# A fifth double step in the third pair of an attention and SwiGLU kernel, with the last quads' attention two visits earlier

## The chip, the cores and the metric

The kernel runs on one core of a Trainium2 chip. The metric is the device time of one execution in microseconds; the median of six runs of the kernel before is 401.4 us.

## What is computed

The reference, cut to its core:

```python
q, k, v: (8, 12, 448, 64)          # batch, heads, sequence, head dimension
attn = sigmoid(q @ k^T / 8 - log(448)) @ v
x = attn, transposed to (8 * 448, 768)
g = x @ w_gate                     # 768 x 1536
out = (g * sigmoid(g) * (x @ w_val)) @ w_out    # w_out: 1536 x 768
```

Attention is elementwise in its sigmoid, so there is no softmax row sum; its output feeds a SwiGLU block. All inputs and the output are float32; inside, the kernel works in bf16 and fp16 with float32 accumulation in PSUM.

## The kernel before, in words

**Attention in quads and visits.** Four heads of one batch form a quad, three quads a batch, 24 quads in all (`NQ`, numbered n). A quad has seven tiles c of 64 keys for each head. For one tile, QK^T (L254) makes 128 x 896 scores in PSUM, and ScalarE's sigmoid (L273, or L270 in two halves) writes them as fp16 into `pt_a`, a ring of ten tiles. When all seven tiles of a quad are there, `pv` (L289) multiplies them with v into one PSUM tile, and VectorE casts the two halves out as `xT` (L304, L312), the transposed input of the block.

Attention is cut into visits: tiles 0 to 3 of a quad, then tiles 4 to 6. The first visit of quad n also runs `pv` of quad n - 1. A visit is put between two units of matrix work of the block.

**The block in pairs of batches.** The eight batches make four pairs pb = 0 to 3. For each pair FFN1 goes over f = 0 to 11, blocks of 128 columns of w_gate and w_val. An ordinary step `ffn1(b, f)` is 12 matmuls for one batch (L324: six for gate, six for value), then a sigmoid on ScalarE (L347) and two VectorE operations (L349, L353) that give `hT`. The pair's FFN2 (L618) follows in four groups of 42 matmuls, or three; it works by a scheme of seven products in place of eight on sums of hT (the S tiles, L539) and sums of w_out.

**Double steps.** For the f listed in `FAST`, FFN1 too uses such a scheme. `double(pb, (f, f + 1))` treats two batches, and gate and value, as a 2 x 2 block product and makes it of seven products of three matmuls, for two f: 42 matmuls (L445) in place of 48. It needs four sums of x (`x_sums`, on GpSimd, L418 to L421) and four sums of weights for each slice of three f (`fast_w`, on VectorE, L397; kind 1 is written in place over w_val). ScalarE copies partial results out (`snap`, L455) and makes two SiLUs; VectorE adds and multiplies (L468, L481, L485, L487, L490). In the kernel before the third pair (pb = 2) has f 0 to 7 in four double steps and f 8 to 11 as ordinary steps, ahead of the double steps; the fourth pair has all twelve f in six double steps. Weight sums and S sums are issued inside double steps as `extra` and by `make_sums`.

**PSUM.** All users share a ring of four tiles of two banks (`ring`, `Banked`). A user that comes round to a tile waits for those that read it last. FFN2 keeps its tile for a whole group.

**Queues.** SyncE issues the loads of q and k, the DMA transposes of the cast q and k (L211), and the stores. GpSimd casts q and k (L204), issues the loads of v, and makes the x sums. What a visit triggers there stands in `plan`: after visit (n, 4), with its sigmoids done (`behind_visit`), quad n + 2 is cast and transposed, its v is loaded, and q and k of quad n + 4 are loaded.

**The order** on each engine is fixed by hand: the units (steps, double steps, parts of FFN2) have nominal durations `FU1` to `FU4`; `PACE` gives nominal times to quads, and a loop puts the next visit ahead of the first unit that starts after its time, if enough nominal time has passed since the last visit:

```python
if visits and tcur >= vtime[0] and not (...) and (vtime[0] < FIRST + 4 or since > (3.8 if len(visits[0]) > 3 else 2.0)):
    seq.append((None, visits.pop(0), 0 if fn is ffn1 else 1))
```

In FFN1 of the second pair this gives a visit of four tiles, a step, a visit of three tiles, two steps, and so on: three steps for a quad. Its 24 steps start with quad 10; quad 18's first visit stands between its last step and FFN2. FFN2 of the second pair holds the visits up to (20, 4), and FFN1 of the third pair those of quads 21 to 23 among its eight ordinary steps.

Of the kernel before, what the change touches and what calls it, by code (L numbers as in the profile page):

```python
# [20 lines left out]
def kernel(  # L21
# [20 lines left out]
    NQ = B * NJ  # L42
    W2 = 2 * S
    LAST = B // 2 - 1
    FAST = {LAST - 1: range(0, 8), LAST: range(NF)}
    hsc = lambda pb: 512.0 if pb in FAST else 4096.0

    qkscale = 1.0 / math.sqrt(D)
# [319 lines left out]

    gT = {}

    def fast_w(s, kind, i=None):

        js = slice(0, JT) if i is None else slice(i, i + 1)
        b11, b21 = wg16[s][:, 0::2][:, js], wg16[s][:, 1::2][:, js]
        b12, b22 = wv16[s][:, 0::2][:, js], wv16[s][:, 1::2][:, js]
        if (s, kind) not in gT:
            n = JT * FW * 128
            at = {3: 0, 2: 1, 4: 2}.get(kind)
            if kind == 1:
                t = wv16[s][:, 0::2]  # L380
            elif s == 0:
                t = half_of(stg_a)[:, at * n:(at + 1) * n]
            elif s == 1 and kind == 3:
                t = half_of(ramp_a)[:, 8 * FW * hw:8 * FW * hw + n]
            elif s == 1:
                t = pt_f[:, (at - 1) * n:at * n]
            elif s == 2:
                t = pt_f[:, (at + 2) * n:(at + 3) * n]
            else:
                t = osp.tile([128, DM], FP32, tag="osb", name=f"g{kind}").bitcast(FP16)[:, :n]  # L390
            gT[(s, kind)] = t if kind == 1 else t.rearrange("p (j n) -> p j n", j=JT)
        t = gT[(s, kind)][:, js]
        a, b, op = {
            3: (b22, b12, SUB), 1: (b12, b11, SUB), 2: (b22, gT.get((s, 1), gT[(s, kind)])[:, js], SUB),
            4: (b21, gT.get((s, 2), gT[(s, kind)])[:, js], SUB),
        }[kind]
        (V if i is None else G).tensor_tensor(out=t, in0=a, in1=b, op=op)  # L397

    pt_f = pt_a.rearrange("p a b s -> p (a b s)")

# [25 lines left out]
    def double(pb, fs, extra=()):  # L426

        b0, b1 = 2 * pb, 2 * pb + 1
        Ds = [Banked("f", made=(pb, f)) for f in fs]
        k = hsc(pb)  # L430
        x = lambda b, odd: lambda j: xT[(b, 2 * j + odd)]
        xs = lambda n: lambda j: xS[(pb, j)][n - 1]
        w = lambda t, odd: lambda f, j: t[f // FW][:, 2 * j + odd, f % FW * 128:(f % FW + 1) * 128]
        ws = lambda kind: lambda f, j: gT[(f // FW, kind)][:, j, f % FW * 128:(f % FW + 1) * 128]
        prods = {
            1: (w(wg16, 0), x(b0, 0)), 2: (w(wg16, 1), x(b0, 1)), 3: (w(wv16, 1), xs(4)), 4: (ws(4), x(b1, 1)),
            5: (ws(1), xs(1)), 6: (ws(2), xs(2)), 7: (ws(3), xs(3)),
        }

        def mm(p, bank, start, stop):  # L440
            for f, D in zip(fs, Ds):
                for j in range(JT):
                    W, X = prods[p]
                    D.write(
                        nc.tensor.matmul(  # L445
                            out=D.t[:, bank, :S], lhsT=W(f, j), rhs=X(j), start=(start and j == 0),
                            stop=(stop and j == JT - 1), skip_group_check=True,
                        ),
                        bank,
                    )  # L450
                yield f, D

        def snap(D, bank, scale, pool, tag):
            o = pool.tile([128, 2, S], FP16, tag=tag, name="snap").rearrange("p a b -> p (a b)").bitcast(FP32)
            D.read(nc.scalar.mul(out=o, in_=D.t[:, bank, :S], mul=scale), bank)  # L455
            return o

        def small(tag):
            return qkT.tile([128, 2, S], FP16, tag=tag, name="small").rearrange("p a b -> p (a b)")

        s1, s2, s5, g, t, v = {}, {}, {}, {}, {}, {}
        for f in fs:
            hT[(pb, f)] = htp.tile([128, 2, S], FP16, tag="hT", name=f"hT_{pb}_{f}")
        for f, D in mm(1, 0, True, False):
            s1[f] = snap(D, 0, 1.0, c16, "c16")
        for f, D in mm(2, 1, True, True):
            g[f] = small("T0").bitcast(FP32)
            D.read(V.tensor_tensor(out=g[f], in0=D.t[:, 1, :S], in1=s1[f], op=ADD), 1)  # L468
        for fn in extra:
            fn()  # L470
        for f, D in mm(6, 0, False, False):
            s2[f] = snap(D, 0, k, v16p, "v16")
        for f in fs:
            t[f] = small("T1")
            nc.scalar.activation(out=t[f][:, :S], in_=g[f], func=SILU)
        for f, D in mm(5, 1, True, False):
            s5[f] = snap(D, 1, k, c16, "c16")
        for f, D in mm(7, 0, False, False):
            v[f] = [tmp.tile([128, S], FP16, tag=tag, name="v") for tag in ("s16", "t1")]
            D.read(  # L480
                V.scalar_tensor_tensor(out=v[f][1], in0=D.t[:, 0, :S], scalar=k, in1=s5[f], op0=MULT, op1=ADD), 0  # L481
            )
        for f, D in mm(3, 1, False, True):
            D.read(
                V.scalar_tensor_tensor(out=v[f][0], in0=D.t[:, 1, :S], scalar=k, in1=s2[f], op0=MULT, op1=ADD), 1  # L485
            )
# [193 lines left out]
    def ffn2_part(pb, moves, by="", extra=()):  # L680

        extra = list(extra)
        for g in moves:
# [3 lines left out]
            if extra:  # L687
                extra.pop(0)()

    FU1, FU2, FU3, FU4 = 2.26, 3.9, 6.83, 7.85  # L690
    units = []
    f1_start, f1_end = {}, {}
    tt = 0.0
    for pb in range(B // 2):
# [8 lines left out]
        for f in FAST.get(pb, ())[::2]:  # L703
            extra = {
                (LAST - 1, 0): ((0, 4), (1, 2)), (LAST - 1, 2): ((1, 4), (2, 3)),
                (LAST - 1, 4): ((2, 1), (2, 2)), (LAST - 1, 6): ((2, 4),),
                (LAST, 0): ((3, 3),), (LAST, 2): ((3, 1),), (LAST, 4): ((3, 2),), (LAST, 6): ((3, 4),),
            }.get((pb, f), ())
            units.append((FU4, double, (pb, (f, f + 1), [lambda a=a: fast_w(*a) for a in extra])))
            tt += FU4  # L710
# [13 lines left out]
        elif pb == 1:  # L724
            part((0, 1, 0, 1), "1")
            part((0,) * 5)
            part((1,) * 5, "", (lambda: list(rest_sums(1, G)),))
            for g in (2, 3):
                part((g,) * 3)
                part((g,) * 4)  # L730
        else:
            part((0, 1) * 7, "1", (skip, lambda: keep_rest(LAST, range(NF), nc.scalar.copy)) if pb < LAST else ())
            if pb == LAST:
                part((3,) * 7)
            part((2,) * 7)
# [2 lines left out]


    FIRST = f1_end[0] - 5.0  # L740
    PACE = ((2 * NJ, FIRST + 3.5), (3 * NJ - 1, FIRST + 28.9), (3 * NJ - 0.5, f1_end[1] - 0.1), (3 * NJ, FIRST + 40.5), (3 * NJ + 2, FIRST + 55.6), (6 * NJ, f1_end[B - 5] - 1.0), (6 * NJ + 0.5, f1_end[B - 5]), (NQ, f1_end[B - 5] + 1.0))
    tiles = [(n, c) for n in range(NJ, NQ) for c in range(C)]
    visits = [tiles[:2], tiles[2:4]]
    for i in range(0, len(tiles), C):
# [173 lines left out]
        plan[(n, 4)] = ((behind_visit, n), (ready, n + 2), (load_v, n + 2)) + ((load_qk, n + 4),) * (n + 4 < NQ)  # L918


    def sums_of_x(pb):
        for j in range(NJ):
            for f in x_sums(pb, j):
                f()

    plan[(NQ - 3, 4)] += ((sums_of_x, LAST - 1),)

    seq = []
    tcur = 3 * FU1
    since, was_v = 99.0, 9  # L930
    was, was_args = ffn1, (0, 2)
    for dur, fn, args in units:
        if visits and tcur >= vtime[0] and not (was is ffn2_part and len(set(was_args[1])) > 1) and not (was is ffn1 and was_args[0] < 2 and was_args[1] == 0) and (vtime[0] < FIRST + 4 or since > (3.8 if len(visits[0]) > 3 else 2.0)):
            seq.append((None, visits.pop(0), 0 if fn is ffn1 else 1))
            vtime.pop(0)
            since, was_v = 0.0, 0
# [6 lines left out]
    for i, (fn, args, _) in enumerate(seq):  # L943
        if fn is ffn1:
            ahead = [len(a) if f is None else 0 for f, a, _ in seq[i + 1:i + 3]] + [0, 0]
            budget[args] = 0 if args == (2 * LAST - 1, 9) else 3 if ahead[0] else 0 if ahead[1] == 4 else 2
        if fn is double:
            args[2].append(lambda: make_sums(5))

# [2 lines left out]
    for fn, args, how in seq:  # L952
# [13 lines left out]
        if pend and (fn is ffn1 and args[1] == 0 and (args[0], NP - 1) not in xT or fn is double or how):  # L966
            for n in pend:
                pv(n)
            pend = []
        if fn is ffn1 and args == (2 * LAST - 2, 8):  # L970
            w2 = [lambda a=a: fast_w(*a) for a in ((1, 3), (1, 1), (0, 3), (0, 1), (0, 2))]
            fill.update({args: w2[:2], (2 * LAST - 1, 10): w2[2:4], (2 * LAST - 1, 11): w2[4:]})
        fn(*args)
        if fn is ffn1 and args == (1, 10):
            behind(hS[last_s[0]][:, :1])
# [44 lines left out]
```

## Time and profile before

| | |
|---|---|
| median of 6 runs | 401.4 us (401.23 to 401.99) |
| the profiled execution, and its span | 401.49 us, 399.7 us |
| DVE, ACT, POOL busy | 250.3, 234.8, 124.3 us |
| FFN1 steps, L324 | 672 matmuls, 148.0 us busy |
| double steps, L445 | 420 matmuls |
| sigmoids of attention, L273 | 148 of 920 ns |
| weight sum of 1152 columns, L397 | about 750 ns |
| S sum of 384 columns, L539 | about 350 ns |
| x sum, L418 to L421 | about 1035 ns |
| granted TensorE clock | 1.00 throughout |

The profile is one execution. Times in its views count from the start of the span; the 1.8 us by which the execution is longer than the span lie around it. Busy shares overlap between engines, so they don't add up; what sets the end is read from the chain that ended last. In a timeline row the columns are start, duration, engine, line, operation, result and operands, and in brackets the idle time ahead of it and what ended that. FFN1 of the second pair runs from about 125 to 204 us, its FFN2 to 239, ordinary steps of the third pair to 267, its double steps from 268 to 300.

### The profile page before, as it was taken

What the parts mean: (1) busy time and instruction counts of PE and PEld (TensorE: products, weight loads), DVE (VectorE), ACT (ScalarE), POOL (GpSimd) and SP (SyncE); (2) the same over time, 40 slices, a digit from 0 to 9 for tenths busy, and PEclk for the clock granted to TensorE, in tenths of its full rate; (3) what the DMA queues carried; (4) which work ended last, traced back from release to release, by engine and by line L of the source; (5) the groups of instructions that cost most, each with busy time, mean ns of one, the idle gap of its engine ahead of it and who ended that gap; (6) DMA issues with size and microseconds to landing.
All of it is one profiled execution on the core that took longest, in us unless ns stands there. A gap on an engine that the chain in (4) does not pass through costs nothing.

```text
span 399.7 us, 8097 instructions
## 1 busy us (share of the span) xinstructions
PE 388.4 (97%) x3116; PEld 201.9 (51%) x3116; DVE 250.3 (63%) x499; ACT 234.8 (59%) x379; POOL 124.3 (31%) x203
## 2 busy tenths in 40 slices
PE   6799999999999999999999999999999999999995
PEld 2345544445555444444455554445556555555653
DVE  2637646688643444466665556479896568887553
ACT  5966785746456777777752667785754055756000
POOL 3629042422311333333333943920007500000900
PEclk9999999999999999999999999999999999999999
DMA  8999979899599777778974899400000520000055
GB/s 248 258 242 259 247 153 252 171 187 120 139 281 233 172 152 172 163 162 100 225 162 105 218 234 171 55 2 0 3 0 2 157 79 2 1 2 0 2 167 149
DMA packets 65575, 54.39 MB, mean 136 GB/s; under 512 B 36033, under 2 KB 61729, under 8 KB 65537
## 3 DMA queue, kind: packets, MB, share of 16 engines
q1 hardware_dynamic: 49744, 38.22, 37.8%
q0 software_dynamic: 15360, 15.34, 24.3%
q8 instruction: 24, 0.39, 0.4%
q10 hardware_dynamic: 432, 0.33, 0.3%
q14 instruction: 15, 0.11, 0.1%
HBM read 47.19 MB, written 11.01 MB: 146 GB/s over the span
## 4 chain that ended last, share of the span: by engine, by line
PE 93%; DMA 3%; DVE 1%; ACT 1%; issue 0%; SPq 0%; POOL 0%; DVEq 0%; ACTq 0%
PE ps_D L324 33%; PE ps_D L618 24%; PE ps_D L445 20%; PE ps_D L289 8%; PE ps_D L254 8%; DMA v<-in_v_dram 2%; DMA st<-in_q_dram 1%; PE ps_D L223 0%; DVE xT L304 0%; DVE xT L312 0%; DVE T L229 0%; ACT pt_a L273 0%; ACT osb L629 0%; DVE t L349 0%; DVE osb L631 0%
## 5 line engine op out<-in xcount | busy, mean ns | idle before, releaser
L273 ACT ACTIVATE pt_a<-ps_D 128x896 f16<-128x896 f32 x148 | 127.3, 920 | 46.8 <-PE ps_D L254 45.8
L324 PE MATMUL ps_D<-xT,wg 128*128 128x448 f16 x336 | 74.3, 353 | 0.3
L324 PE MATMUL ps_D<-xT,wv 128*128 128x448 f16 x336 | 73.7, 352 | 0.0
L349 DVE TENSOR_TENSOR t<-ps_D,s 128x448 f16<-128x448 f32 x56 | 34.9, 624 | 52.0 <-ACT s L347 50.9
L324 PEld LDWEIGHTS <-wg 128*128 128x128 f16 x336 | 30.2, 98 | 36.3 <-issue 12.1
L324 PEld LDWEIGHTS <-wv 128*128 128x128 f16 x336 | 32.8, 98 | 31.0 <-issue 0.6
L455 ACT ACTIVATE snap<-ps_D 128x448 f32<-128x448 f32 x60 | 31.2, 542 | 28.1 <-PE ps_D L445 26.4
L254 PE MATMUL ps_D<-T,T 64*64 64x448 bf16 x644 | 44.3, 357 | 2.1 <-DVE T L229 1.0
L347 ACT ACTIVATE s<-ps_D 128x448 f16<-128x448 f32 x56 | 30.9, 551 | 24.3 <-PE ps_D L324 22.5
L204 POOL CAST c<-stg_a 128x896 bf16<-128x896 f32 x40 | 36.4, 936 | 15.9 <-DMA stg_a<-in_q_dram 14.1
L618 PEld LDWEIGHTS <-S 128*128 128x128 f16 x312 | 30.2, 98 | 20.9 <-issue 1.3
L618 PE MATMUL ps_D<-ramp_a,S 128*128 128x384 f16 x234 | 40.2, 326 | 0.0
L353 DVE SCALAR_TENSOR_TENSOR hT<-ps_D,t 128x448 f16<-128x448 f32 x56 | 35.0, 625 | 5.8
L289 PE MATMUL ps_D<-pt_a,v 64*64 64x448 f16 x672 | 36.0, 350 | 0.9 <-DMA v<-in_v_dram 0.8
L636 DVE SCALAR_TENSOR_TENSOR osb<-ps_D,osb 128x384 f32<-128x384 f32 x42 | 23.4, 557 | 20.0 <-PE ps_D L618 14.6
L631 DVE TENSOR_SCALAR osb<-ps_D 128x384 f32<-128x384 f32 x39 | 21.7, 557 | 20.3 <-PE ps_D L618 16.9
L828 POOL CAST held<-S 128x1 bf16<-128x1 f16 x3 | 0.6, 188 | 100.4 <-ACT osb L629 55.7
L828 POOL CAST held<-pt_a 128x1 bf16<-128x1 f16 x13 | 2.5, 189 | 93.2 <-ACT pt_a L273 93.2
L618 PEld LDWEIGHTS <-hT 128*128 128x128 f16 x228 | 22.1, 98 | 15.6 <-issue 1.3
L254 PEld LDWEIGHTS <-T 64*64 64x64 bf16 x644 | 15.1, 105 | 24.6 <-issue 17.8
L304 DVE CAST xT<-ps_D 128x448 f16<-128x448 f32 x21 | 13.1, 625 | 22.4 <-PE ps_D L289 19.3
L289 PEld LDWEIGHTS <-v 64*64 64x64 f16 x672 | 19.5, 107 | 13.8 <-DMA v<-in_v_dram 1.2
(108 smaller groups left out, 497.1 us busy)
## 6 DMA issues: line engine op xcount, KB each, us to landing
out_dram<-osb SPq DMA_DIRECT2D x52, 192.0 KB, 3.3
stg_a<-in_q_dram SPq DMA_DIRECT2D x18, 448.0 KB, 5.6
stg_a<-in_k_dram SPq DMA_DIRECT2D x18, 448.0 KB, 6.2
v<-in_v_dram POOLq DMA_DIRECT2D x36, 112.0 KB, 4.5
wg<-in_moe_w_gate_dram POOLq DMA_DIRECT2D x4, 576.0 KB, 12.4
wv<-in_moe_w_val_dram POOLq DMA_DIRECT2D x4, 576.0 KB, 13.1
wo<-in_moe_w_out_dram POOLq DMA_DIRECT2D x4, 576.0 KB, 8.8
v<-in_v_dram POOLq DMA_DIRECT2D x6, 224.0 KB, 10.7
```

Source lines behind the costliest of these rows:

```text
L204: eng.tensor_copy(out=t.rearrange("p c h d -> p h c d"), in_=st.rearrange("p h (c d) -> p h c d", c=C))
L254: nc.tensor.matmul(out=sc[g:g + 64, h2, :S], lhsT=kt[r, w * 64:(w + 1) * 64], rhs=qt[r, :, w * 64:(w + 1) * 64], start=True, stop=True,)
L273: nc.scalar.activation(out=pt, in_=sc[:, :, :S], func=SIGM, bias=sbias, scale=qkscale)
L289: nc.tensor.matmul(out=P[g:g + 64, h2, :S], lhsT=vt[r, h2, c * D:(c + 1) * D], rhs=pt[r, h2, :], start=(c == 0), stop=(c == C - 1),)
L324: nc.tensor.matmul(out=D.t[:, i, :S], lhsT=(wg16, wv16)[i][f // FW][:, pr, cs], rhs=xT[(b, pr)], start=(pr == 0), stop=(pr == NP - 1),),
L347: D.read(nc.scalar.activation(out=s16, in_=D.t[:, 0, :S], func=SIGM), 0)
L349: D.read(nc.vector.tensor_tensor(out=t1, in0=D.t[:, 0, :S], in1=s16, op=MULT), 0)
L353: nc.vector.scalar_tensor_tensor(out=hT[(b // 2, f)][:, b % 2, :], in0=D.t[:, 1, :S], scalar=hsc(b // 2), in1=t1, op0=MULT, op1=MULT),
L445: nc.tensor.matmul(out=D.t[:, bank, :S], lhsT=W(f, j), rhs=X(j), start=(start and j == 0), stop=(stop and j == JT - 1), skip_group_check=True,
L455: D.read(nc.scalar.mul(out=o, in_=D.t[:, bank, :S], mul=scale), bank)
L618: nc.tensor.matmul(out=D.t[:, bank, :hw], lhsT=l, rhs=B_(i), start=(first and i == order[0]), stop=(i == order[-1]), skip_group_check=True,),
L636: D.read(nc.vector.scalar_tensor_tensor(out=o, in0=i, scalar=1.0 / hsc(pb), in1=o, op0=MULT, op1=ADD), bank)
```

## The change

- f 8 and 9 of the third pair become a fifth double step. The pair keeps f 10 and 11 as ordinary steps: four where there were eight.
- `PACE` moves quads 18 and later one quad on relative to the nominal end of FFN1 of the second pair, and the loop's minimum distance ahead of a four-tile visit falls from 3.8 to 2.0 from quad 12 on. In the order that results, FFN1 of the second pair holds 15 visits from (12, 0) on where it held 13: (12, 0) to (18, 4), with (19, 0) between its last step and FFN2. FFN2 of the second pair holds the visits up to (21, 4), FFN1 of the third pair those of quads 22 and 23, one ahead of each step. Between (11, 4) and (13, 0) stand three steps, and four between (n, 4) and (n + 2, 0) elsewhere in this stage; before there were five.
- The fourth slice of weights is cut in two for its sums (`gcut`): f 9 alone (384 columns a sum), f 10 and 11 (768 columns). The sums for f 9 are made in double steps of the third pair, for f 10 and 11 in the fourth pair.
- Two weight sums of the second slice move from FFN1 of the third pair into FFN2 of the second pair, group 3; the x sums of the third pair are issued after FFN2 of the second pair and not by `plan` of quad 21.
- One special budget of S sums goes.

```diff
-    FAST = {LAST - 1: range(0, 8), LAST: range(NF)}
+    FAST = {LAST - 1: range(0, 10), LAST: range(NF)}
...
+    gcut = [(i, 0, FW) for i in range(NW - 1)] + [(NW - 1, 0, 1), (NW - 1, 1, FW)]
+    def gpart(f):
+        return next(i for i, (s, lo, hi) in enumerate(gcut) if s == f // FW and lo <= f % FW < hi)
+    def fast_w(i, kind):
+        s, lo, hi = gcut[i]
+        cs = slice(lo * 128, hi * 128)
+        b11, b21 = wg16[s][:, 0::2, cs], wg16[s][:, 1::2, cs]
+        b12, b22 = wv16[s][:, 0::2, cs], wv16[s][:, 1::2, cs]
+        n = JT * (hi - lo) * 128
...
+            elif i == 3:
+                o = JT * FW * 128 * 5 + NF * 128
+                t = pt_f[:, o + at * n:o + (at + 1) * n]
...
+        V.tensor_tensor(out=t, in0=a, in1=b, op=op)
...
-                (LAST - 1, 4): ((2, 1), (2, 2)), (LAST - 1, 6): ((2, 4),),
-                (LAST, 0): ((3, 3),), (LAST, 2): ((3, 1),), (LAST, 4): ((3, 2),), (LAST, 6): ((3, 4),),
+                (LAST - 1, 4): ((2, 1), (2, 2)), (LAST - 1, 6): ((2, 4), (3, 3), (3, 1), (3, 2)),
+                (LAST - 1, 8): ((3, 4),),
+                (LAST, 0): ((4, 3),), (LAST, 2): ((4, 1),), (LAST, 4): ((4, 2),), (LAST, 6): ((4, 4),),
...
-            for g in (2, 3):
-                part((g,) * 3)
-                part((g,) * 4)
+            part((2,) * 3)
+            part((2,) * 4)
+            part((3,) * 3, "", (skip, lambda: fast_w(1, 3), lambda: fast_w(1, 1)))
+            part((3,) * 4)
+            o_units.append((0.0, sums_of_x, (LAST - 1,)))
...
-    PACE = (..., (6 * NJ, f1_end[B - 5] - 1.0), (6 * NJ + 0.5, f1_end[B - 5]), (NQ, f1_end[B - 5] + 1.0))
+    PACE = (..., (6 * NJ + 1, f1_end[B - 5] - 1.0), (6 * NJ + 1.5, f1_end[B - 5]), (NQ, f1_end[B - 5] + 1.0))
...
-    plan[(NQ - 3, 4)] += ((sums_of_x, LAST - 1),)
...
-        if visits and ... since > (3.8 if len(visits[0]) > 3 else 2.0)):
+        if visits and ... since > (3.8 if len(visits[0]) > 3 and visits[0][0][0] < 4 * NJ else 2.0)):
...
-            budget[args] = 0 if args == (2 * LAST - 1, 9) else 3 if ahead[0] else 0 if ahead[1] == 4 else 2
+            budget[args] = 3 if ahead[0] else 0 if ahead[1] == 4 else 2
...
-        if fn is ffn1 and args == (2 * LAST - 2, 8):
-            w2 = [lambda a=a: fast_w(*a) for a in ((1, 3), (1, 1), (0, 3), (0, 1), (0, 2))]
-            fill.update({args: w2[:2], (2 * LAST - 1, 10): w2[2:4], (2 * LAST - 1, 11): w2[4:]})
+        if fn is ffn1 and args == (2 * LAST - 2, 10):
+            w2 = [lambda a=a: fast_w(*a) for a in ((0, 3), (0, 1), (0, 2))]
+            fill.update({(2 * LAST - 1, 10): w2[:2], (2 * LAST - 1, 11): w2[2:]})
```

More of the change, by code (lines that the diff above doesn't have):

```diff
@@ L369 @@
     gT = {}
[L371 to L381, printed above, removed]
+    gcut = [(i, 0, FW) for i in range(NW - 1)] + [(NW - 1, 0, 1), (NW - 1, 1, FW)]
@@ new lines, in gpart @@
+    def gpart(f):
[6 more added lines that the diff above has]
+        n = JT * (hi - lo) * 128
+        at = {3: 0, 2: 1, 4: 2}.get(kind)
+        if kind == 1:
+            t = b12
+        else:
+            if i == 0:
@@ L382, in fast_w @@
                 t = half_of(stg_a)[:, at * n:(at + 1) * n]
-            elif s == 1 and kind == 3:
+            elif i == 1 and kind == 3:
                 t = half_of(ramp_a)[:, 8 * FW * hw:8 * FW * hw + n]
-            elif s == 1:
+            elif i == 1:
                 t = pt_f[:, (at - 1) * n:at * n]
-            elif s == 2:
+            elif i == 2:
                 t = pt_f[:, (at + 2) * n:(at + 3) * n]
+            elif i == 3:
+                o = JT * FW * 128 * 5 + NF * 128
+                t = pt_f[:, o + at * n:o + (at + 1) * n]
@@ L389, in fast_w @@
             else:
                 t = osp.tile([128, DM], FP32, tag="osb", name=f"g{kind}").bitcast(FP16)[:, :n]
-            gT[(s, kind)] = t if kind == 1 else t.rearrange("p (j n) -> p j n", j=JT)
-        t = gT[(s, kind)][:, js]
+            t = t.rearrange("p (j n) -> p j n", j=JT)
+        gT[(i, kind)] = t
         a, b, op = {
-            3: (b22, b12, SUB), 1: (b12, b11, SUB), 2: (b22, gT.get((s, 1), gT[(s, kind)])[:, js], SUB),
-            4: (b21, gT.get((s, 2), gT[(s, kind)])[:, js], SUB),
+            3: (b22, b12, SUB), 1: (b12, b11, SUB), 2: (b22, gT.get((i, 1)), SUB), 4: (b21, gT.get((i, 2)), SUB),
@@ L396, in fast_w @@
         }[kind]
-        (V if i is None else G).tensor_tensor(out=t, in0=a, in1=b, op=op)
+        V.tensor_tensor(out=t, in0=a, in1=b, op=op)
     pt_f = pt_a.rearrange("p a b s -> p (a b s)")
@@ L433, in double, with ws, at @@
         w = lambda t, odd: lambda f, j: t[f // FW][:, 2 * j + odd, f % FW * 128:(f % FW + 1) * 128]
-        ws = lambda kind: lambda f, j: gT[(f // FW, kind)][:, j, f % FW * 128:(f % FW + 1) * 128]
+        def ws(kind):
+            def at(f, j):
+                i = gpart(f)
+                lo = (f % FW - gcut[i][1]) * 128
+                return gT[(i, kind)][:, j, lo:lo + 128]
+            return at
         prods = {
@@ L688, in ffn2_part, with sums_of_x @@
                 extra.pop(0)()
+    def sums_of_x(pb):
+        for j in range(NJ):
+            for f in x_sums(pb, j):
+                f()
     FU1, FU2, FU3, FU4 = 2.26, 3.9, 6.83, 7.85
@@ L740 @@
     FIRST = f1_end[0] - 5.0
-    PACE = ((2 * NJ, FIRST + 3.5), (3 * NJ - 1, FIRST + 28.9), (3 * NJ - 0.5, f1_end[1] - 0.1), (3 * NJ, FIRST + 40.5), (3 * NJ + 2, FIRST + 55.6), (6 * NJ, f1_end[B - 5] - 1.0), (6 * NJ + 0.5, f1_end[B - 5]), (NQ, f1_end[B - 5] + 1.0))
+    PACE = ((2 * NJ, FIRST + 3.5), (3 * NJ - 1, FIRST + 28.9), (3 * NJ - 0.5, f1_end[1] - 0.1), (3 * NJ, FIRST + 40.5), (3 * NJ + 2, FIRST + 55.6), (6 * NJ + 1, f1_end[B - 5] - 1.0), (6 * NJ + 1.5, f1_end[B - 5]), (NQ, f1_end[B - 5] + 1.0))
     tiles = [(n, c) for n in range(NJ, NQ) for c in range(C)]
@@ L918 @@
         plan[(n, 4)] = ((behind_visit, n), (ready, n + 2), (load_v, n + 2)) + ((load_qk, n + 4),) * (n + 4 < NQ)
[L921 to L924, printed above, removed]
-    plan[(NQ - 3, 4)] += ((sums_of_x, LAST - 1),)
     seq = []
@@ L932 @@
     for dur, fn, args in units:
-        if visits and tcur >= vtime[0] and not (was is ffn2_part and len(set(was_args[1])) > 1) and not (was is ffn1 and was_args[0] < 2 and was_args[1] == 0) and (vtime[0] < FIRST + 4 or since > (3.8 if len(visits[0]) > 3 else 2.0)):
+        if visits and tcur >= vtime[0] and not (was is ffn2_part and len(set(was_args[1])) > 1) and not (was is ffn1 and was_args[0] < 2 and was_args[1] == 0) and (vtime[0] < FIRST + 4 or since > (3.8 if len(visits[0]) > 3 and visits[0][0][0] < 4 * NJ else 2.0)):
             seq.append((None, visits.pop(0), 0 if fn is ffn1 else 1))
```

## The prediction

> **What bounds the kernel now.** I read the page first, then the chain that ended last, then the timelines at three places that the change alters.
>
> ```profile
> PE 388.4 (97%) x3116; PEld 201.9 (51%) x3116; DVE 250.3 (63%) x499; ACT 234.8 (59%) x379; POOL 124.3 (31%) x203
> ...
> PE 93%; DMA 3%; DVE 1%; ACT 1%; issue 0%; SPq 0%; POOL 0%; DVEq 0%; ACTq 0%
> ```
>
> TensorE works 97% of the span and carries 93% of the chain. A matmul removed shortens the end; a wait added to TensorE lengthens it. In order of time the chain prices every unit that the change moves:
>
> ```profile
> 137.15 0.69 PE ps_D L254 x12
> 137.84 4.65 PE ps_D L324 x24
> 142.49 0.50 PE ps_D L254 x8
> 142.99 1.32 PE ps_D L289 x28
> 144.31 0.38 PE ps_D L254 x8
> 144.69 2.38 PE ps_D L324 x12
> ...
> 268.06 31.89 PE ps_D L445 x168
> ```
>
> The visit to a quad's last three tiles costs 0.69 us; the visit to the first four, with the earlier quad's PV inside, 0.50 + 1.32 + 0.38 = 2.20. One FFN1 step behind a visit costs 2.38, a second one 4.65 - 2.38 = 2.27. Four double steps of 42 matmuls take 31.89, 7.97 each. I write (n,0) for the visit to tiles 0 to 3 of quad n and (n,4) for the one to tiles 4 to 6.
>
> **The gain.** Four steps become one double step: 4 x 2.27 = 9.08 against 7.97, so -1.11 us (six matmuls of 0.19 give the same). The number of visits stays, so their cost moves and doesn't change.
>
> **First new wait: quad 13's transposes.** Before, five FFN1 steps always stand between (n,4), whose plan casts and transposes quad n+2, and (n+2,0), which reads it. The order of the changed kernel has four, and between (11,4) and (13,0) only three. On TensorE that stretch is 0.69 + 2.38 + 2.20 + 2.38 + 0.69 + 2.38 = 10.72 us. The other chain, in the timeline from (11,4) on:
>
> ```profile
> 137.08 0.76 PE L254 MATMUL ps_D<-T,T 64*64 64x448 bf16 x12
> 137.52 2.54 ACT L273 ACTIVATE pt_a<-ps_D 128x896 f16<-128x896 f32 x3 [0.67 <-PE ps_D L254]
> ...
> 139.92 0.56 ACT L347 ACTIVATE s<-ps_D 128x448 f16<-128x448 f32 x1
> ...
> 140.30 1.81 POOL L204 CAST c<-stg_a 128x896 bf16<-128x896 f32 x2
> ...
> 141.25 0.62 DVE L353 SCALAR_TENSOR_TENSOR hT<-ps_D,t 128x448 f16<-128x448 f32 x1
> 141.26 1.28 SPq L211 DMA_TRANSPOSE T<-c  x1
> ```
>
> Three sigmoids, then the hold behind them, two casts, two transposes. The second is issued at 142.64 (the first at 141.26, 1.28 of issue and a gap of 0.1). Its own entry in the view of tile T, and that of the slowest one, at 182.4:
>
> ```profile
> DMA to landing us min/median/max: 5.8/5.8/5.8
> ```
> ```profile
> DMA to landing us min/median/max: 7.3/7.3/7.3
> ```
>
> So k of quad 13 lands at 148.44, while TensorE wants it at 137.08 + 10.72 = 147.80. With about 0.1 for the semaphore and the weight load, the wait is 0.7 us. The same entry reads 5.2 in the slots at 152.5 and 172.3; that would make it 0.1. 7.3 would make it 2.2. I take 5.8: up to 140.15 this very slot has the same instructions in both kernels. All other shortened stretches have four steps, 13.0 us against 11.4, and keep over 1.5 us; a stall at quad 13 only adds to that. The next narrowest is quad 23: the slot that will hold its second transpose lands at 239.92 + 5.9 = 245.8, and (23,0) is due at 239.12 + 2.20 + 2.38 + 0.69 + 2.38 = 246.77. 1.0 us is left; no cost, but 0.5 at 7.3.
>
> The Trainium skill, "DMA: Bandwidth & Descriptors", section "Issuing engines are not separate DMA queues", says that transfers issued by SP and POOL run on the same 16 DMA engines and interleave. This speaks against closer visits, since the loads of one quad then run into the transposes of the next; at 182.4 the v, q and k transfers of that slot are as late as its transposes, which fits. The page gives no price for it.
>
> **Second new wait: the start of FFN2 of the second pair.** Before, two FFN1 steps run ahead of the last visit, (18,0); after, (18,4), one step, (19,0). The second FFN2 group takes the PSUM buffer that held the PV result, and its first matmul waits for both DVE casts out of it (ps_D_99 in the order of both kernels). Before:
>
> ```profile
> 202.36 0.62 DVE L353 SCALAR_TENSOR_TENSOR hT<-ps_D,t 128x448 f16<-128x448 f32 x1
> ...
> 204.03 0.62 DVE L304 CAST xT<-ps_D 128x448 f16<-128x448 f32 x1 [0.24 <-PE ps_D L289]
> ...
> 204.57 0.61 DVE L312 CAST xT<-ps_D 128x448 f16<-128x448 f32 x1
> ```
>
> With the visit's start at 202.08 as zero, the casts end at 3.10, and the group begins at 3.20 (2.20 for the visit, 0.98 for the first group's six matmuls): 0.1 to spare. After, the last gate follows a three-tile visit, as at 137.08 above: there hT starts 4.17 after that visit, which is 4.17 - 3.07 = 1.10 after the next one. Three S sums follow on DVE (0.54, 0.92 and 1.20 after hT's start, as at 192.44), the casts start 1.47 and 2.01 after it, and the second ends at 1.10 + 2.01 + 0.61 = 3.72. TensorE waits 3.72 + 0.07 - 3.20 = 0.59 us. Bounds: 0.50 and 0.65, by the semaphore and DVE's spacing.
>
> **Smaller waits.** In the first double step s5's copy (ACT L455) ended 0.08 ahead of the matmul that needs its bank, of which 0.05 is the semaphore. Upstream, DVE's `small` started at 270.47, 2.81 after hT's at 267.66. Now the two S sums in between depend on the hT just made and on each other, where before one was ready: 0.66, 1.05, then 1.32 (weight sum), 1.99 and 2.53 (casts), 3.07. That is 0.26 late; less the slack, 0.18 (0.1 to 0.25). In the double step for f 6, 7, DVE has four weight sums (one of 1152 columns, three of 384) and four S sums between `small` and L481, where the busiest one had two and four and left 0.08 us. By rows (1152: 0.75, 384: 0.35) and the waits among the three I get 3.0 to 3.3 us of room needed from 294.92 and 3.2 available: 0 to 0.15, I take 0.05. One stall goes: the 0.09 before the second step behind a three-tile visit (at 167.7), a place that a visit now breaks up.
>
> The skill's "VectorE: DVE Perf Modes", section on the TRN2 errata, holds that an SBUF operation pays a fixed cost per instruction, and advises tiles of 512 and more, which speaks against cutting a weight sum of 1152 into 384 and 768. The rows agree in kind: 0.75 and 0.35 make 0.15 fixed. Its expression (58 + half the columns at 0.96 GHz) gives an estimate of 0.26 for 384 columns; by that the double step for f 6, 7 would not wait at all.
>
> **What costs nothing, and its cover.** POOL's 12 x-sums (1.03 each, 12.4) start at about 240.6, wait for the stores of FFN2's last group (landing by 247.6) and end before 254; the first double step is due at 239.12 + 16.75 = 255.9 and reads them 2.3 later. Each us beyond 4 of delay would be paid. The two weight sums put into FFN2's fourth group (0.75 each) push one PSUM copy by 0.3, and that bank is next written after a 0.69 visit and a 0.98 product. The closer visits' sigmoids: the sequence four-tile visit, step, three-tile visit, step, four-tile visit stood already at 44 to 57 us, where the chain is PE alone. Loads of q and k have two quads' time (over 20 us) against 6.2 to land, and SP keeps transposes ahead of the fourth group's stores as before. The fifth double step in itself is like the others.
>
> **The sum** against the profiled execution's 401.49 (span 399.7 and 1.8 around it, 0.1 above the median of 401.4): -1.11 - 0.09 + 0.70 + 0.59 + 0.18 + 0.05 = +0.32. On the median: 401.7 us.
>
> **Rivals.**
> A (forecast, 0.60): the gain is paid back in waits; with 5.2 to 5.9 at quad 13 and the smaller bounds, -0.5 to +0.65, 400.9 to 402.1.
> B, the covers hold (0.15): quad 13's transposes land at 5.2 or sooner and FFN2's casts are not needed so early, so 0.3 us of waits remain: 401.4 - 0.9 = 400.5. For: of the thirteen slots from 119 us on, ten have 5.1 to 5.6 for the second transpose. Against: the FFN2 wait is made of DVE rows that hardly vary.
> C, slower (0.25): the transposes of the closer quads land late, as at 182.4. Quad 13 then waits 2.2 (1.5 more), quad 23 0.5: 401.7 + 1.5 to 2.0, about 403.4. It decides from 6.3 us to land, where the total passes +0.8. For: the DMA share is 0.80 over 122 to 205 us, at 9.92 us for a quad; at 7.65 it is full. Against: quad 13's slot itself has yet no closer neighbour.
> That the change would not do what it says is out: the order shows 3110 matmuls for 3116, and (19,0) ahead of FFN2.
>
> **The numbers.** A measurement of this kernel tells 0.2%, 0.8 us, from no change: 400.6 to 402.2. A gives 0.57 to no change and 0.03 to slower, B 0.10 to faster and 0.05 to no change, C 0.21 to slower and 0.04 to no change: faster 0.10, same 0.66, slower 0.24. Range for 8 in 10: 400.6 (B's middle) to 403.0 (C's lower part).
>
> **What would show it.** Matmuls of L445 x462 in all, the page's count 3110; in the chain a DMA piece of T ahead of L254 at about 148 (quad 13), 0.1 to 0.8 long, and a DVE xT piece ahead of L618 at about 208; a short ACT snap piece in the first double step at about 257; no POOL xS piece. Wrong if neither wait shows and the span is 398.6, or if transposes stand in the chain at several quads.

## The result, and the profile after

The changed kernel took 402.67 us (median of 16 runs, 402.11 to 404.22) beside 401.49 for the kernel before (37 runs): ratio 1.0031, 95% interval 1.0024 to 1.0037, so 1.2 us slower. Compared again with the same kernel before on two other occasions, it was at 1.0017 (1.0008 to 1.0025) and 1.0022 (1.0012 to 1.0031). It is slower each time, by 0.7 to 1.2 us, about at the 0.2% that I had called the limit of what can be told. The forecast of 401.7 with "no change" as the likeliest case was too low by one microsecond; the time lies in the upper part of the stated range, 400.6 to 403.0.

The matmuls are gone as foreseen, in the first line of busy times:

```profile
PE 388.7 (97%) x3110; PEld 201.6 (50%) x3110; DVE 253.0 (63%) x505; ACT 237.5 (59%) x385; POOL 123.6 (31%) x203
```

TensorE's busy time nevertheless rose from 388.4 to 388.7. A second profile of the kernel before (before_again below) has 391.1, so the busy times of the page don't tell where the loss is. The chain that ended last, in order of time (start, length, what), holds the larger ones:

```profile
208.91 0.54 DVE xT L312
209.45 0.04 issue
209.50 7.97 PE ps_D L633 x48
...
260.21 4.66 PE ps_D L460 x24
264.87 0.03 ACTq L470
264.90 0.65 ACT small L490 x2
265.55 0.44 ACT snap L470
265.99 0.04 issue
266.04 34.21 PE ps_D L460 x180
300.25 20.48 PE ps_D L633 x126
320.72 47.67 PE ps_D L460 x252
...
380.26 3.31 DMA out_dram<-osb
...
383.69 0.57 DVE osb L646
384.26 0.04 issue
384.30 11.87 PE ps_D L633 x72
```

Three places where TensorE is released by another engine, where the chain of before was TensorE alone: the start of FFN2 of the second pair (209.50), the first double step (266.04) and the last FFN2, where a copy waits for a store to land (384.30). The first two were in the forecast, the third was not.

A table of stages says what each is worth. It counts from the first matmul of the second pair's FFN1, because the start-up ahead of that varies between executions: in the 14 profiles of this study that matmul starts anywhere from 124.2 to 126.0 us. The stages are taken from the starts of TensorE's matmuls in the trace; the last one ends with its last matmul.

| us | before | before, again | changed | changed, again | changed, third |
|---|---|---|---|---|---|
| FFN1, 2nd pair | 79.59 | 79.59 | 83.08 | 83.09 | 83.08 |
| FFN2, 2nd pair | 36.97 | 36.97 | 37.65 | 37.66 | 37.65 |
| ordinary steps, 3rd pair | 26.73 | 26.73 | 14.66 | 14.66 | 14.67 |
| double steps, 3rd pair | 31.79 | 31.79 | 39.94 | 39.95 | 39.94 |
| FFN2, 3rd pair | 20.48 | 20.48 | 20.48 | 20.47 | 20.48 |
| double steps, 4th pair | 47.67 | 47.67 | 47.67 | 47.67 | 47.67 |
| FFN2, 4th pair | 27.46 | 27.46 | 27.93 | 27.57 | 28.22 |
| from the start of FFN1, 2nd pair, to the end of the span | 275.01 | 275.02 | 275.73 | 275.39 | 276.05 |

Outside the last FFN2 the stages repeat to 0.01 us. The first six rows sum to +0.25 us, the last FFN2 adds 0.11 to 0.76: 0.4 to 1.0 in the spans.

### The profile page after: what moved, and what is told of

Same layout as the page of the kernel before. It is cut to its first block, busy times and chain, and to the rows that moved or that the text cites. A ratio compares the mean times of both kernels' runs of the same rounds, so it can differ in the third digit from the quotient of the medians.

```text
span 400.5 us, 8109 instructions
## 1 busy us (share of the span) xinstructions
PE 388.7 (97%) x3110; PEld 201.6 (50%) x3110; DVE 253.0 (63%) x505; ACT 237.5 (59%) x385; POOL 123.6 (31%) x203
## 5 line engine op out<-in xcount | busy, mean ns | idle before, releaser
L324 PE MATMUL ps_D<-xT,wg 128*128 128x448 f16 x312 | 69.2, 353 | 0.2
L324 PE MATMUL ps_D<-xT,wv 128*128 128x448 f16 x312 | 68.5, 352 | 0.0
L349 DVE TENSOR_TENSOR t<-ps_D,s 128x448 f16<-128x448 f32 x52 | 32.4, 624 | 53.6 <-ACT s L347 53.1
L470 ACT ACTIVATE snap<-ps_D 128x448 f32<-128x448 f32 x66 | 34.1, 541 | 29.5 <-PE ps_D L460 27.6
L324 PEld LDWEIGHTS <-wg 128*128 128x128 f16 x312 | 27.8, 98 | 34.0 <-issue 12.1
L324 PEld LDWEIGHTS <-wv 128*128 128x128 f16 x312 | 30.4, 98 | 28.8 <-issue 0.6
L347 ACT ACTIVATE s<-ps_D 128x448 f16<-128x448 f32 x52 | 28.7, 552 | 22.8 <-PE ps_D L324 21.1
L353 DVE SCALAR_TENSOR_TENSOR hT<-ps_D,t 128x448 f16<-128x448 f32 x52 | 32.5, 625 | 5.4
L460 PE MATMUL ps_D<-xS,wv 128*128 128x448 f16 x132 | 28.6, 352 | 0.0
L460 PE MATMUL ps_D<-xT,wg 128*128 128x448 f16 x132 | 26.8, 353 | 0.0
```

The source lines that it names most:

```text
L324: nc.tensor.matmul(out=D.t[:, i, :S], lhsT=(wg16, wv16)[i][f // FW][:, pr, cs], rhs=xT[(b, pr)], start=(pr == 0), stop=(pr == NP - 1),),
L347: D.read(nc.scalar.activation(out=s16, in_=D.t[:, 0, :S], func=SIGM), 0)
L349: D.read(nc.vector.tensor_tensor(out=t1, in0=D.t[:, 0, :S], in1=s16, op=MULT), 0)
L353: nc.vector.scalar_tensor_tensor(out=hT[(b // 2, f)][:, b % 2, :], in0=D.t[:, 1, :S], scalar=hsc(b // 2), in1=t1, op0=MULT, op1=MULT),
L460: nc.tensor.matmul(out=D.t[:, bank, :S], lhsT=W(f, j), rhs=X(j), start=(start and j == 0), stop=(stop and j == JT - 1), skip_group_check=True,
```

## The experiments

The theory after the first profile: the step's 1.11 us is paid back by waits that the closer visits make (FFN2's start, and small ones at many visits) plus something at the end. The rivals: transposes that land late in unprofiled executions (C of the prediction), and a double step that is worth less than its matmuls in that place.

**casts_first**, the FFN2 wait alone. The S sums of the last step are not issued behind the step, and so come behind the casts:

```diff
-            budget[args] = 3 if ahead[0] else 0 if ahead[1] == 4 else 2
+            budget[args] = 0 if args == (2 * LAST - 3, NF - 1) else 3 if ahead[0] else 0 if ahead[1] == 4 else 2
```

> The changed kernel with one reordering on DVE: the three S sums behind the last FFN1 step of the second pair are held back, so that the two casts xT of the last visit's PV result come ahead of them. If the wait at the start of FFN2 is a real price of the closer visits (my second term, 0.59; the trace of the changed kernel shows 0.52 of idle TensorE there and a first FFN2 stretch of 9.56 us for 8.88), the idle time goes and the first stretch falls back to about 8.9: 0.5 to 0.7 us below the changed kernel, 402.0 on the median and span 399.9. Rival 1, the wait only hides another one behind it (a store of that group, the next PSUM bank): the gap moves by less than 20 us and the time stays at 402.6. Rival 2, the loss comes from transposes that land late in some executions: the time stays at 402.4 to 402.7 and its spread stays as wide (402.1 to 404.2).

Measured 401.64 us (ratio 1.0000, 0.9991 to 1.0008), FFN2 of the second pair 36.96. Its chain has no cast at FFN2's start any more, and it has quad 13's transposes:

```profile
142.40 5.41 DMA T<-c
147.81 0.04 issue
147.85 0.57 PE ps_D L254 x8
...
207.75 8.89 PE ps_D L633 x54
```

The first stretch of FFN2 is 8.89 us again for 54 matmuls, as before the change. For comparison, the chain of the kernel before:

```profile
204.36 8.90 PE ps_D L618 x54
```

So the wait is shown, at 0.69, and nothing hides behind it. Rival 1 falls with that. This one profile lost 0.35 of the gain elsewhere: FFN1 of the second pair took 83.25 for 83.08 (the wait for quad 13's transposes) and the last FFN2 28.11 for 27.93. The median fell by more than 0.69 and the spread narrowed (401.3 to 402.2), so that rival 2, a second cause in unprofiled executions, was not out of the question: the changed kernel itself had to be measured again. Against its later two ratios the step is 0.7 to 0.9, which leaves little for it.

**visits_alone**, the visits of the changed kernel, but four double steps:

```diff
-    FAST = {LAST - 1: range(0, 10), LAST: range(NF)}
+    FAST = {LAST - 1: range(0, 8), LAST: range(NF)}
-    gcut = [(i, 0, FW) for i in range(NW - 1)] + [(NW - 1, 0, 1), (NW - 1, 1, FW)]
+    gcut = [(i, 0, FW) for i in range(NW)]
```

and the weight sums in the double steps as in the kernel before.

> The changed kernel's visit positions with four double steps as before, so four ordinary FFN1 steps in place of the fifth double step. If the double step itself is worth its 1.11 us and the loss comes from the visits (FFN2 start 0.6 to 0.7, seven or eight visits at 0.08 to 0.12 each, perhaps 0.5 at the end), this kernel is slower than the kernel before by 1.2 to 1.9 us, 402.7 to 403.4, and 0.9 to 1.1 above the changed kernel less what the first double step loses there (0.1 to 0.2). If instead the double step is worth much less in that place (its weight sums and copies hold it up), this kernel is about as fast as the changed one, 402.4 to 402.7, that is 0.9 to 1.2 above before. If the visits cost nothing, it is within 0.2 of before.

Measured 404.04 us (1.0052, 1.0040 to 1.0065), slower than any theory allowed. The chain ahead of its first double step runs through VectorE:

```profile
268.37 0.68 DVE stg_a L402
...
271.83 0.73 DVE stg_a L402
272.56 0.05 issue
272.61 29.68 PE ps_D L457 x156
```

Weight sums stand there beside four ordinary steps that no longer have visits between them, and TensorE idles for 1.06 us. That was the edit's own fault, and it decides nothing about the visits; visits_alone_2 mends it.

**quad13_later**, one more step ahead of quad 13's two visits:

```diff
+    at_13 = next(i for i, g in enumerate(visits) if g[0] == (13, 0))
+    vtime[at_13] = max(vtime[at_13], f1_start[2] + 8 * FU1 - 0.1)
+    vtime[at_13 + 1] = max(vtime[at_13 + 1], f1_start[2] + 9 * FU1 - 0.1)
```

> The changed kernel with the two visits of quad 13 one FFN1 step later, so that four steps stand between (11,4) and (13,0) as at the other quads, and one of the seven tight places (three-tile visit, one step, four-tile visit) is gone. If the transposes of quad 13 bind in most executions but not in the profiled one (rival C or my first term at 0.70), the median falls by 0.3 to 0.8 from the changed kernel's, to 401.9 to 402.4, and the spread narrows to the 0.9 us that most executions keep. If they don't bind, only the tight visit's 0.08 goes: 402.5 to 402.6, the same spread.

Measured 402.13 us (1.0009, 1.0000 to 1.0018). FFN1 of the second pair took 83.00, 0.08 less: the price of one tight place (three-tile visit, a single step, four-tile visit) and no more. The median alone fitted the late transposes; a repeat beside the changed kernel follows below (quad13_again).

**spread_visits**, positions by hand for quads 10 to 19, in steps from the start of FFN1:

```diff
+    starts = (0, 2, 5, 8, 10, 13, 16, 18, 21, 24)
+    for i, grp in enumerate(visits):
+        n, c = grp[0]
+        if 10 <= n <= 19 and (n, c) < (19, 1):
+            vtime[i] = f1_start[2] + (starts[n - 10] + (c > 0)) * FU1 - 0.1
```

Besides, the loop's minimum distance of 3.8 ahead of a four-tile visit now ends with quad 9 and not with quad 11.

> The changed kernel with the visits of quads 10 to 19 placed by hand, three FFN1 steps to a quad: four-tile visit, one step, three-tile visit, two steps; only three places keep the tight pattern, every (n,4) has at least four steps to (n+2,0), and two steps stand ahead of the last visit (19,0). The same number of visits and steps as in the changed kernel. If the loss is the sum of the FFN2 wait (0.6 to 0.7) and of the tight visits at 0.08 (four of seven go, 0.3), it falls by 0.9 to 1.0, to 401.6, the time before; with the wait at the end of the run gone too, if that is chance, to 401.2. If the tight visits cost nothing of their own, it is 402.0. If the loss is at the double step, it stays at 402.5.

Measured 401.45 us (0.9996, 0.9985 to 1.0006). FFN1 of the second pair 82.75 (four tight places fewer, 0.33 less, so 0.08 each), its FFN2 36.96 (the wait gone by the order of the visits alone). Both prices of the theory stand.

**changed_again**, the changed kernel with no edit.

> The changed kernel itself, once more, beside the next three. Its runs lay 1.2 us above the kernel before, and its one profile 0.8 above, while holding back three S sums took 1.2 off where the profile's idle time was 0.66. If the waits seen in single profiles come and go by chance (quad 13's transposes, absent in the first profile and 0.17 with the sums held back; the store at the end, 0.31 and 0.49), another profile of the same kernel shows another mix of them, with a span between 400.0 and 400.9, and the median is 0.7 to 1.2 above before. If the first measurement stands as it is, the median is again 1.1 to 1.4 above and a wait that neither profile shows is to be looked for.

Measured 402.15 us (1.0017). The two waits that vary are indeed absent from its chain: quad 13's product starts only 0.09 late, and the last FFN2 is one piece, 0.11 longer than before the change:

```profile
368.35 27.42 PE ps_D L633 x168
```

**visits_alone_2**, visits_alone with the weight sums moved beside visits:

```diff
-        if fn is ffn1 and args == (2 * LAST - 2, 10):
+        if fn is ffn1 and args == (2 * LAST - 2, 9):
...
-            fill.update({(2 * LAST - 1, 10): w2[:2], (2 * LAST - 1, 11): w2[2:]})
+            fill.update({args: w2[:1], (2 * LAST - 2, 10): w2[1:2], (2 * LAST - 2, 11): w2[2:]})
```

> The closer visits with four double steps, as in visits_alone, but the three weight sums that stood on DVE beside the last two ordinary steps of the third pair (with no visit next to them there, they kept TensorE idle for 1.06 us ahead of the first double step) are put beside the visits of quads 22 and 23. If that pile-up was a fault of my experiment, the gap goes and the kernel is 1.3 us above before (0.50 + 0.68 + 0.12 from the stages), 402.8 to 403.1; the changed kernel less this one is then what the fifth double step brings, net of its own waits: -1.11 + 0.20 + 0.3 to 0.5 at the end, -0.4 to -0.6. If the pile-up stays (S sums alone suffice), it is again 402.1 in span and 2.1 above before.

Measured 402.74 us (1.0030, 1.0018 to 1.0042), 1.27 above before. In its chain the pile-up is gone:

```profile
259.86 9.19 PE ps_D L324 x48
269.04 31.78 PE ps_D L457 x168
...
368.97 27.31 PE ps_D L630 x168
```

Four ordinary steps and four double steps take 9.19 + 31.78 = 40.97 us, where the changed kernel's chain has 300.25 - 260.21 = 40.04 for its five: the fifth double step is worth 0.93, about its 1.11 less 0.20 at the first double step. The theory that it is worth less falls. In time the changed kernel beside it is 0.59 faster, within the 0.4 to 0.6 expected; the visits cost 1.28 in the span (276.29 for 275.01), and the last FFN2 has no wait with four double steps.

**stores_split**, two queues for the first stores of the last FFN2:

```diff
-            store((nc.sync, nc.sync), *rows[0], o1, both)
+            store((nc.sync, nc.scalar if pb == LAST and g < 2 else nc.sync), *rows[0], o1, both)
```

> The changed kernel with one edit at the end: of the two halves of the first stores of groups 0 and 1 in the last FFN2, ScalarE's queue issues the second (SyncE's issued both). In all four kernels with five double steps the second of these issues takes 0.91 to 1.34 us, in both kernels with four 0.59; the copy that needs the buffer waits for its landing, and TensorE for the copy (0.31 idle in the changed kernel). If the serial issue on SyncE is the cause, the idle time goes and the last FFN2 falls from 27.9 to 27.5 us: 0.3 to 0.5 below the changed kernel run beside it. If the landing itself is late in these kernels whatever issues it, the last FFN2 stays at 27.7 to 28.1.

Measured 402.10 us (1.0021, 1.0011 to 1.0030), no gain over the changed kernel beside it. The last FFN2 fell to 27.46, but the time from its last matmul to the end rose from 4.32 to 4.59, and changed_again, profiled beside it, had little wait to lose (0.11). In time the edit is inconclusive.

**spread_split**, spread_visits with the split stores and, by the same means as in casts_first, the S sums of the last ordinary step of the third pair held back.

> All that the stages point to together: the visits spread by hand (as in spread_visits), the split stores of stores_split, and the S sums of the last ordinary step of the third pair held back, so that the first double step finds the PV casts done (0.20 us there in each kernel with five double steps). From spread_visits' span of 399.63: less 0.5 at the end (gap) and 0.2 at the first double step, 398.9 to 399.1, and a median of 400.7 to 400.9, 0.8 to 1.0 below before. If the held sums only move the wait into a later double step, 401.0; if the store stays late, 401.3.

Measured 400.77 us (0.9987, 0.9978 to 0.9996), 0.7 below before and the fastest version of the study. Its chain has a plain FFN2 start, five double steps at 7.97 and a plain end:

```profile
206.98 8.90 PE ps_D L633 x54
...
258.61 39.83 PE ps_D L460 x210
...
366.59 27.32 PE ps_D L633 x168
```

**before_again**, the kernel before with no edit, as a control.

> The kernel before, timed against itself and profiled once more. It prices two things: what the comparison makes of no change (ratio 1.000, within 0.1%), and whether its last FFN2 (27.46 us, no wait for a store) and its quad 13 vary from execution to execution. If a store's issue of 0.9 us or more near 380 us is a matter of chance in any kernel, it can show here too; if it belongs to five double steps, this profile has issues of 0.47 to 0.60 again, as the two kernels with four have had so far.

Measured 401.79 us, ratio 1.0003 (0.9992 to 1.0015): no change is told as no change. Its stages are in the table, its store issues in the last FFN2 take 0.47 to 0.60.

**changed_third** and **quad13_again**, side by side.

> The changed kernel a third time; its two comparisons gave 1.2 and 0.7 us above before, its profiles 0.8 and 0.4. What stays in every profile (tight visits 0.60, FFN2 start 0.68, quad 23 0.12, first double step 0.20, less 1.11 and 0.09) is 0.4; the rest comes and goes. If that is all, the median is again 0.5 to 1.2 above before, and the profile's span 400.1 plus whatever chance wait it holds at quad 13 (0 to 0.2) or at the end (0 to 0.5).

> quad13_later beside the changed kernel on one chip. In six profiles with quad 13 early its second transpose landed at most 0.1 us ahead of the product that needs it, and 0.17 behind the need in one. If it is late by more in many unprofiled executions (rival C), this kernel's median is 0.5 or more below the changed kernel's of the same call; if the wait is the 0 to 0.2 that the profiles show, 0.1 to 0.3 below (0.08 of it the tight visit).

Measured 402.42 us for both, with ratios of 1.0022 (1.0012 to 1.0031) and 1.0014 (1.0005 to 1.0023). The medians are equal and the ratios differ by 0.3 us, well within their intervals. That speaks against late transposes that cost unprofiled executions half a microsecond or more; with 12 runs of each kernel it doesn't exclude it.

**spread_held**, spread_split without the split stores.

> spread_split without the split stores: visits spread by hand and the S sums of the last ordinary step of the third pair held back, SyncE issues all stores. If the split stores were worth the 0.5 us of the end wait, it is 401.2 to 401.3, half a microsecond above spread_split; if that wait is chance, 400.8 to 401.0. Either way 0.2 to 0.7 below before.

Measured 401.35 us (0.9993, 0.9982 to 1.0004). From the start of FFN1 of the second pair its span is 274.48, 0.53 below before; spread_split's is 274.32. The first matmul of that FFN1 came the latest of all profiles, 1.3 us behind the first one's, which hides the gain in the span. The last FFN2 was 27.89 here and 27.46 with split stores, a longer end takes back 0.27 of that. Only spread_split is faster than before beyond its interval.

## Why the prediction was right or wrong

**The gain, -1.11: right.** 40.97 against 40.04 us is 0.93, and the 0.20 of the first double step comes on top.

**FFN2's start, +0.59: right in place and cause, small by 0.1.** The stage grew by 0.68.

**The first double step, +0.18: right, 0.20.** The chain has the short ACT pieces that were expected, though from 264.90 and not at about 257. This double step starts at 260.14, not at the 255.9 of the prediction, which had left out that two visits now stand ahead and that the waits add up (3.49 and 0.68 in the table); the copy comes 5.3 us into it. Holding the sums back takes the wait away (39.74 in spread_held and spread_split for 39.94). The 0.05 at f 6, 7 did not appear: every later double step takes 7.94.

**Quad 13, +0.70: wrong in size.** The step that failed is the landing. Timeline and tile view of the changed kernel:

```profile
147.92 0.57 PE L254 MATMUL ps_D<-T,T 64*64 64x448 bf16 x8
```
```profile
DMA to landing us min/median/max: 4.8/4.8/4.8
```

I had taken 142.64 + 5.8 = 148.44 against a need at 147.80 to 147.9. The second transpose was issued later, at 143.05, but landed 4.8 after that, at 147.82, just in time. In the three profiles of the changed kernel it took 4.6 to 5.0. The product started 0.29 us after the step's last matmul in two of them and 0.37 in changed_again, where 0.28 is usual: waits of 0.01 and 0.09, the latter in place of a 0.08 described below. In casts_first the landing took 5.4 and TensorE idled for 0.17. These are about the lower of my bounds, 0.1. The reason I gave for the middle one, the same instructions in the slot before the change, doesn't reach far enough: this slot has 5.8 and 6.3 in the two profiles of the kernel before. What else makes the difference, no run isolates. **Rival C** goes with it. Over 119 to 243 us the transposes of the changed kernel land in

```profile
DMA to landing us min/median/max: 3.0/4.8/6.6
```

against 5.2 and 7.3 for median and maximum before. Closer visits did not make them later. The rule that I had set beside this (the Trainium skill, "DMA: Bandwidth & Descriptors", section "Issuing engines are not separate DMA queues", on transfers that interleave on the same engines whoever issues them) may hold, but no run here shows it costing the transposes anything.

**"What costs nothing": wrong by 0.7 us for the closer visits.** The x sums, the two weight sums and the fifth double step were free as foreseen: none of them stands in the chain. But I had let the closer visits pass because the same sequence stood at 44 to 57 us, where the chain is TensorE alone. The row that I leaned on had the price in it. From the chain of before:

```profile
45.95 0.38 PE ps_D L254 x8
...
52.27 1.32 PE ps_D L289 x28
53.60 0.46 PE ps_D L254 x8
54.05 2.38 PE ps_D L324 x12
```

The visit at 51.77 is the one behind the tight pattern, and its last piece is 0.46 instead of 0.38. So short a wait stays inside the chain's TensorE piece and only makes it longer. The cause is in the timeline of the changed kernel:

```profile
167.69 0.56 ACT L347 ACTIVATE s<-ps_D 128x448 f16<-128x448 f32 x1
168.28 0.62 DVE L349 TENSOR_TENSOR t<-ps_D,s 128x448 f16<-128x448 f32 x1 [2.48 <-ACT s L347]
168.31 1.49 PE L289 MATMUL ps_D<-pt_a,v 64*64 64x448 f16 x28
169.01 0.62 DVE L353 SCALAR_TENSOR_TENSOR hT<-ps_D,t 128x448 f16<-128x448 f32 x1
169.69 0.57 PE L254 MATMUL ps_D<-T,T 64*64 64x448 bf16 x8
```

The step's sigmoid stands behind three attention sigmoids on ScalarE (165.28 to 167.82), so hT is late and ends at 169.63; the visit's second half of QK needs that PSUM tile and starts 0.06 later, 1.38 after PV began instead of 1.32. Seven of the nine visits in that stage pay this. The stage grew by 3.49; the two visits that moved in are 0.69 + 2.20, with 0.11 for each step that now stands first behind a visit 3.11; 0.38 remain. That is seven times 0.08 less the stall that went, which was 0.16 and not my 0.09: before the change 0.44 us lie between the last matmul of the visit (167.25) and the step's first (167.69), where 0.28 is usual. (23, 0) pays another 0.12.

**The end: not in the sum at all.** I costed the last FFN2 at nothing because no edit touches it. It grew by 0.11 to 0.76 in every kernel with five double steps whose stores are issued by SyncE alone (eight profiles), and in no kernel with four (four profiles). The SP timeline shows two issues in 1.68 us after the change, 1.10 before, the second 1.16 instead of 0.59:

```profile
379.74 1.68 SPq L565 DMA_DIRECT2D out_dram<-osb  x2
```
```profile
379.44 1.10 SPq L550 DMA_DIRECT2D out_dram<-osb  x2
```

What lies beside it is a load of instructions, on queue q8 of the page (24 a run, 0.39 MB). In the DMA view, one load starts between 379.7 and 380.2 of the changed kernel and one between 378.5 and 379.0 of the kernel before:

```profile
q8 instruction: 1, 0.02, 15.7%
```
```profile
q8 instruction: 1, 0.02, 16.6%
```

By the trace's DMA records the one after the change starts at 379.80 and takes 1.25 us; the store's issue ends at 381.42, 0.37 behind it. In all eight profiles the long issue is the one that is open when that load ends, and it ends 0.37 to 0.38 later. In the seven of them where it is the second issue, the growth of the stage is the time of this issue less 0.68 to 0.70: its length reaches TensorE one for one. Counted from the first matmul of the last FFN2 the load starts 10.6 to 10.8 us in with four double steps; with five and SyncE's stores it is 11.5 to 11.7 in six profiles and 12.2 to 12.3 in two. Six matmuls fewer, with their six weight loads, shift TensorE's stream by twelve instructions, about 1.0 us of it, which fits the six. The Trainium skill, "Runtime: NRT & Kernel Launch", section "Instruction fetch mechanics", says that an engine's instructions are refilled in 16 KiB blocks of 256, and calls the cost of a block "mostly hidden". The blocks agree: 24 of 0.39 MB in all would be 6144 instructions, and TensorE has 3110 matmuls and as many weight loads. The cost does not: TensorE doesn't starve, but another engine's issue takes up to 0.9 longer. That the load belongs to TensorE's stream shows in the traces: in all 14 profiles it starts when TensorE has begun 6027 to 6037 matmuls and weight loads, with four double steps (6029 to 6031) as with five, and no other engine has more than 700 instructions. That it holds the issue is argued from the times; no run moved the load alone.

So the terms that were named summed to +0.32, and what was found without the end is +0.25. That these are so near is luck: a visit price of 0.7 (0.56 and 0.12) that I had missed took the place of 0.7 at quad 13 that did not come. With the end it is 0.4 to 1.0. The first comparison lies past the border of 0.8 that I had set between "no change" and "slower", the other two about at it. Why the first median is 1.2 above, more than any of the three profiles, stays open. Rival A's mechanism, the gain paid back in waits, is the right one; its size was too small by a place that I had not looked at. B fails by FFN2's start, the visits and the end, although quad 13 went its way.

## What to carry to other kernels

A precedent in the profile proves an edit free only if its own rows are compared with those of an undisturbed neighbour: 0.46 beside 0.38 is easily passed over in a chain that reads "PE alone", and seven such places made half a microsecond. Where a TensorE-bound kernel has little slack, an order that puts a step's sigmoid behind three others and a PSUM reuse straight after it costs at each repetition; spreading the visits by hand gave 0.3 us back and took away the wait at FFN2's start as well. Look also at stages that the edit does not touch: fewer instructions ahead of them shift everything that runs by instruction count.

## What the runs showed of the hardware

A load of 16 KB of instructions takes 0.9 to 1.4 us at this place, and in eight profiles a store issue that was open when it ended lasted until 0.37 us after it: 0.55 to 0.59 became 0.89 to 1.45 us. Where SyncE and ScalarE issue at the same time (spread_split), two issues were open, took 0.91 and 0.89 and ended 0.65 after the load. It is no rule for every issue: in three of the four profiles with four double steps the first issue of the row (0.47) is open at that moment and ends 0.06 to 0.28 after it. Why that one is not held stays open, as does the later load in two of the eight profiles (6 and 8 TensorE instructions behind the usual place).

From the first matmul of the second pair's FFN1 on, two executions of the kernel before agree to 0.01 us in each stage. Their spans differ by 0.51 us, and 0.50 of it lies ahead of that point, in the start-up.
